# Attention followed by a soft mixture of experts on one core: the V products of a pair gathered in one place, x turned later beside them, the batch softmax steps spread out

## The chip, the cores and the metric

The kernel runs on one core of a Trainium2 chip. A core has five engines that work side by side, each through its own queue in order: TensorE (PE: matrix products and transposes through the array, results in PSUM), VectorE (DVE), ScalarE (ACT), GpSimd (POOL) and SyncE (SP). They wait for each other through semaphores. PSUM has eight banks per core; each holds 512 float32 numbers in each of 128 partitions. The metric is the device time of one execution in microseconds (us). All numbers come from one profiled execution of the kernel before and from three timed runs of it.

## What is computed

The first half is an attention whose softmax has an extra one in its denominator, the second half a soft mixture of experts over its result:

```python
# q, k, v: [8, 12, 448, 64] (batch, heads, tokens, width of a head)
scores = scale * q @ k.T
m = max(scores, -1); e = exp(scores - m)
attn = e / (sum(e) + exp(-m) + 1e-9)
x = (attn @ v), heads side by side           # [3584, 768]
logits = x @ phi                              # 32 slots: 8 experts x 4
d = softmax(logits, over the 3584 tokens)     # dispatch
slot_input = d.T @ x                          # [32, 768]
slot_out = relu(slot_input @ w1[e]) @ w2[e]   # per expert
c = softmax(logits, over the 32 slots)        # combine
out = c @ slot_out                            # [3584, 768]
```

## The kernel before

**Pairs, groups, batches, slots.** Two heads make a pair (48 pairs, n = 0..47), three pairs a group (16), six pairs a batch (8, called b). The main loop has a turn s = 0..48 for each pair, called a slot here, in two halves y = 0 and 1; `hs = 2s + y` counts half slots. The order of work on each engine is the order of the text: the schedule is written by hand, no planner reorders it. Different stages of different pairs share a slot:

- `A` (L218): scores for the maxima, some pairs ahead. PE writes scores (L227; the last, half-sized block L237) into a bank of psA, DVE takes the maximum over a row (L231, L240). Seven maxima per slot: the first and second A, two tiles each, lie in half 0, the third (two tiles) and fourth (one) in half 1.
- `W1`, `W2`, `W3`, once per group: POOL negates the maxima (L247), PE turns them (L267, L268), ACT copies them (L273) and makes exp(-m) (L276, L279). W2 and W3 are in half 1 of each slot with s = 2, 5, 8, ...
- `Bk` (L283): scores again for pair s into psB (L302), the negative maximum added by a second product (L305), ACT takes the exponential (L308). Blocks 0 and 1 in half 0 (four exponentials), 2 and 3 in half 1 (three).
- `T` (L195): PE turns q and k of pair s + 6 (28 transposes, L205) into a psA bank, in half 1; ACT copies it out for the first pair of a group (L208), DVE for the other two (L210).
- `AV` (L327): the V products of a pair (L339), 24 for the three full blocks of queries and 8 for the half-sized one (index 3), summed in one bank of psV. The blocks i = 0, 1 of keys are multiplied in half 1 of the pair's own slot, the rest in half 0 of the next.
- `N1` (L345): ACT copies the sums out (L351). `N2` (L354), in half 1 of the slot after the pair's: DVE makes the divisors (L360, L361), POOL multiplies (L367, L375, L376) and so writes x.
- `PX` (L390): PE turns x of pair s - 2 (four products, L399) into a psB bank, in half 1, and ACT copies it (L405) to xT.
- `P(b)` (L413): the steps of the batch softmax. l_mm makes the logits of the batch (24 products L434; ACT copy L438, DVE maximum L442); l_turn turns them (L450, L452) and c_sub subtracts on POOL (L457); s_max spreads the maxima (L462 to L465), d_sub subtracts on POOL (L469); exps takes exponentials on ACT (L474, L479) and corr rescales the sums on POOL (L480); s_mm sums d.T @ x (28 products L489, DVE sum L499); c_turn turns c (L494, L495). `late(b)` is true for b < 6.

**Banks.** psA has three banks for scores for maxima, T and the steps of P; psB has four for Bk, W2 and PX; psV one. A tile takes the bank of the tile three (four, one) before it, and PE waits until that one has been read.

**Other work of POOL.** POOL also copies V into place (L314 to L317, at the end of slots 0, 3, 6, ...) and issues all loads: v (L145, L146), q and k (L141), the experts' weights (L108). Behind the loop the last batch's steps, the experts and the output follow; the change does not touch these, apart from where they begin.

The positions of the steps of P in half slots, counted from slot 6b + 8, are 0, 1, 2, 4, 6, 9 (s_mm last) for late batches, and 0, 1, 2, 4, 5, 7 for b = 6.

Of the kernel before, what the change touches and what calls it, by code (L numbers as in the profile page):

```python
# [31 lines left out]
def kernel(  # L32
# [20 lines left out]
    PB = H // 2  # L53
    NPAIR = B * PB
# [67 lines left out]
    with ExitStack() as at:  # L122
# [62 lines left out]
        mx, ngm, ec, mT, eT, av, us = {}, {}, {}, {}, {}, {}, {}  # L185
        qkT = {}
        st = {"e2": 0}
# [133 lines left out]
        def av_tile(n):  # L321

            if n >= NPAIR - 3 and n % 2:
                return psA.tile([128, 512], F32, tag="a", name="ps_av")
            return psV.tile([128, 512], F32, tag="v", name="ps_av")

        def AV(n, i, qs):  # L327
            g, pl = divmod(n, NP)
            if i == 0 and qs[0] == 0:
                av[n] = av_tile(n)  # L330
            a = av[n]
            for u in qs:
                for hl in range(2):
                    if u < 3:
                        c0 = (2 * u + hl) * W65
                        o, qc = a[:, c0:c0 + W65], slice(u * 128, (u + 1) * 128)
                    else:
                        o, qc = a[64 - 64 * hl:128 - 64 * hl, 6 * W65:7 * W65], slice(384, 448)
                    nc.tensor.matmul(o, eT[n, i, hl][:, qc], vp[g % 2][:, 2 * pl + hl, i, 0:W65],  # L339
                                     start=(i == 0 and u == 0 and hl == 0),  # L340
                                     stop=(i == 3), skip_group_check=True)

        on_pool = lambda n: n < NPAIR - 4

        def N1(n):  # L345
            src = av[n][:, 0:7 * W65].rearrange("p (s c) -> p s c", c=W65)
            if n == NPAIR - 1:
                us[n] = src
                return
            u = ubuf[:, n % 2, :].rearrange("p (s c) -> p s c", c=W65)  # L350
            (nc.scalar.copy if on_pool(n) else nc.vector.tensor_copy)(u, src)  # L351
            us[n] = u

        def N2(n):  # L354
            g, pl = divmod(n, NP)
            b, pb = divmod(n, PB)
            u = us[n]
            eng = nc.gpsimd if on_pool(n) else nc.vector
            rec = psm.tile([128, 7], F32, tag="rec", name="rec", bufs=3)
            nc.vector.scalar_tensor_tensor(rec, u[:, :, D], 1e-9, ec[mg(n)][:, pl, :], op0=ALU.add, op1=ALU.add)  # L360
            nc.vector.reciprocal(rec, rec)  # L361
            x = xb[b % 2]
            c = pb * 128
            rec2 = psm.tile([128, 2], F32, tag="rec2", name="rec2", bufs=3)
            if n == NPAIR - 1:
                nc.vector.tensor_scalar(rec2, halfm, rec[:, 6:7], None, op0=ALU.mult)
            eng.tensor_mul(  # L367
                x[:, 0:3, c:c + 128].rearrange("p i (h d) -> p i h d", h=2),
                u[:, 0:6, 0:D].rearrange("p (i h) d -> p i h d", h=2),
                rec[:, 0:6].rearrange("p (i h) -> p i h", h=2).unsqueeze(3).to_broadcast([128, 3, 2, D]))  # L370
            if n == NPAIR - 1:
                for h in range(2):
                    nc.scalar.mul(x[:, 3, c + 64 * h:c + 64 * h + 64], u[:, 6, 0:D], rec2[:, h:h + 1])
                return
            eng.tensor_scalar(rec2, halfm, rec[:, 6:7], None, op0=ALU.mult)  # L375
            eng.tensor_mul(  # L376
                x[:, 3, c:c + 128].rearrange("p (h d) -> p h d", h=2),
                u[:, 6, 0:D].unsqueeze(1).to_broadcast([128, 2, D]),
                rec2.unsqueeze(2).to_broadcast([128, 2, D]))
# [3 lines left out]
        def keep_busy(n):  # L383

            if "idle" not in st:
                st["idle"] = pb_("ps_idle")
            for _ in range(n):
                nc.tensor.matmul(st["idle"], ident, w_sb["w1", 0][:, 0, 0:512], start=True, stop=True)

        def PX(n):  # L390
            b, pb = divmod(n, PB)
            x, c = xb[b % 2], slice(pb * 128, pb * 128 + 128)
            two = n == NPAIR - 1
            pss = [pb_("ps_x") for _ in range(1 + two)]
            for i in range(4):
                if i == 3 and two:
                    keep_busy(1)
                o = (i % 2 if two else i) * 128
                nc.tensor.matmul(pss[i // 2 if two else 0][:, o:o + 128], x[:, i, c], ident if i < 3 else ident2,  # L399
                                 start=True, stop=True)  # L400
            if two:
                nc.scalar.copy(xT[:, pb, 0:256], pss[0][:, 0:256])
                nc.vector.tensor_copy(xT[:, pb, 256:512], pss[1][:, 0:256])
            else:
                nc.scalar.copy(xT[:, pb, :], pss[0])  # L405
# [4 lines left out]
        late = lambda b: b < B - 2  # L410
# [114 lines left out]

        post = {}
        for b in range(B - 1):
            for z, f in enumerate(P(b)):  # L530
                post[2 * (PB * b + PB + 2) + z + (z > 2) + (z > 3 + (not late(b))) + 2 * (z > 4) * late(b)] = f

        ub = ubuf.rearrange("p n c -> p (n c)").bitcast(BF16)
        take = lambda z, n: ub[:, z:z + n]
# [14 lines left out]
        def As(c):  # L549
            for _ in range(min(c, len(runs))):  # L550
                A(*runs.pop(0))
# [23 lines left out]
        for s in range(NPAIR + 1):  # L575
            for y in range(2):
                hs = 2 * s + y
                early = int(hs < 5)
                As(1)
                if s < NPAIR:  # L580
                    Bk(s, 2 * y)
                    As(early)
                    side = int(y == 1 and len(runs) > 0 and runs[0][1] == 3)
                    Bk(s, 2 * y + 1, side)
                    As(1 - side)
                else:
                    As(1)
                if hs == 1:
                    W1(1)
                if hs < 5:  # L590
                    T(hs + 3)
                if y == 0:
                    if 0 <= s - 1:
                        for i in (2, 3):
                            AV(s - 1, i, range(3))
                else:
                    if 2 <= s < NPAIR - 6:
                        T(s + 6)
                    g = (s + 1) // 3
                    if (s + 1) % 3 == 0 and g < NG:  # L600
                        W2(g + 1)
                        W3(g + 1)
                    if s < NPAIR:
                        for i in (0, 1):
                            AV(s, i, range(3))
                if 2 * s + y in post:
                    post[2 * s + y]()
                if y and 0 <= s - 2 < NPAIR - 2:
                    PX(s - 2)
                if y == 0:  # L610
                    if 0 <= s - 1:
                        for i in range(4):
                            AV(s - 1, i, [3])
                        N1(s - 1)
                        if not on_pool(s - 1):
                            N2(s - 1)
                else:
                    if 0 <= s - 1 and on_pool(s - 1):
                        N2(s - 1)
                As(early)  # L620
                if hs == 1:
                    W2(1)
                    W3(1)
                if hs == 4:
                    W1(2)
            g = (s + 9) // 3
            if s % 3 == 0 and g - 2 < NG:
                V(g - 2)
                if s and g - 1 < NG:
                    load(g - 1, "v")  # L630
            if s == 1 or (s and s % 3 == 0):
                if g < NG:
                    load(g, "q")
                    load(g, "k")
            if s % 3 == 1:
                if 1 < (s + 2) // 3 < NG:
                    W1((s + 2) // 3 + 1)
                if s == 1:
                    load(2, "v")
            if s in half_at:  # L640
                load_half(half_at[s], 0, w_tile(half_at[s]))
            if s - 1 in half_at:
                load_half(half_at[s - 1], 1)
            for i, z0, z1 in part_at.get(s, ()):
                load_part(i, z0, z1)
# [63 lines left out]
        for half in range(2):  # L709
            for bp in range(B // 2):  # L710
                o = (half * (B // 2) + bp) * 4
                nc.tensor.matmul(ps_cs[:, o:o + 4], cT[:, bp, half, :, :].rearrange("p b j -> p (b j)"), band,
                                 start=True, stop=True)
# [7 lines left out]
        for half in range(2):  # L721
            hs = slice(half * ND, (half + 1) * ND)
# [61 lines left out]
```

## Time and profile before

| What | Value |
|---|---|
| Median of three runs | 328.88 us (327.84 to 330.64) |
| The profiled execution, its own time | 327.88 us |
| Its span, first to last instruction | 326.1 us |
| PE busy | 283.2 us, 87% |
| DVE busy | 252.6 us, 77% |
| ACT busy | 251.5 us, 77% |
| POOL busy | 200.3 us, 61% |
| Row maxima, L231 and L240, DVE | 288 of 613 ns, 48 of 615 ns |
| Exponentials L308, ACT | 336, mean 557 ns |
| V products L339, PE | 1536, 65.0 us busy |
| Granted clock of PE in the loop | 1.00 |

The span is the time between the profile's first and last instruction, the execution's time is a little longer than it. Busy times of one engine overlap with those of another, and neighbouring instructions of one engine overlap too (maxima of 0.61 us follow each other every 0.53 us), so that a cadence, from one start to the next, says more than a duration. In a line of the timeline the columns are: start, length of the group, engine, line, operation, written and read tile with their shapes, number of instructions; in brackets the idle time of that engine before it and what ended it.

### The profile page before, as it was taken

To read this page: it belongs to the slowest core of one execution; us is meant where nothing else is said; L and a number is where in the kernel's file an instruction comes from. 1 tells how busy PE (TensorE), PEld (TensorE's weight loads), DVE (VectorE), ACT (ScalarE), POOL (GpSimd) and SP (SyncE) were. 2 spreads that over 40 slices of the span, in tenths; PEclk is the share of its full clock that TensorE was granted. 3 is DMA by queue.
4 is the path that set the end of the run, shared out by engine and by line. 5 is a ranking of instruction groups with operands and counts; after the bars stand their busy time and mean duration, and the time that the engine had idled before them with its cause. 6 is when DMAs were issued, how large, how long until landed. Compare 5 with 4: busy or idle time off the path is not lost.

```text
span 326.1 us, 12146 instructions
## 1 busy us (share of the span) xinstructions
PE 283.2 (87%) x5074; PEld 162.6 (50%) x5074; DVE 252.6 (77%) x575; ACT 251.5 (77%) x546; POOL 200.3 (61%) x402
## 2 busy tenths in 40 slices
PE   2898999999999999899999999999899997977800
PEld 1444465565665566556655665565555554541100
DVE  5789999998798979798989889888798364326910
ACT  2466699999898999899898989898899993306800
POOL 8651778779587959595979597958766823000000
PEclk9999999999999999999999999999999999987555
DMA  6990899999999999569999999999536999963997
GB/s 87 139 134 2 123 207 155 200 178 178 173 153 166 176 187 146 83 88 181 145 196 154 198 140 199 147 196 140 84 50 98 148 158 192 199 111 150 441 422 338
DMA packets 42438, 54.30 MB, mean 166 GB/s; under 512 B 2576, under 2 KB 35344, under 8 KB 42000
## 3 DMA queue, kind: packets, MB, share of 16 engines
q0 software_dynamic: 41376, 42.52, 84.1%
q1 hardware_dynamic: 1008, 11.01, 8.0%
q8 instruction: 39, 0.64, 0.8%
q14 instruction: 15, 0.12, 0.1%
HBM read 85.03 MB, written 11.01 MB: 295 GB/s over the span
## 4 chain that ended last, share of the span: by engine, by line
PE 37%; DVE 17%; POOL 16%; DMA 12%; ACT 7%; issue 6%; POOLq 0%; ACTq 0%; DVEq 0%
DVE mx L231 11%; DMA R<-in_k_dram 8%; PE ps_av L339 8%; PE ps_b L302 7%; PE ps_a L227 5%; PE ps_b L305 5%; DMA R<-in_moe_w_dram 4%; PE ps_t L205 4%; POOL R L141 3%; POOL R L367 2%; ACT R L308 2%; PE ps_o L742 2%; POOL R L247 2%; ACT W L748 2%; DVE mx L240 2%
## 5 line engine op out<-in xcount | busy, mean ns | idle before, releaser
L231 DVE TENSOR_REDUCE mx<-ps_a 128x1 f32<-128x448 f32 x288 | 160.2, 613 | 14.0 <-PE ps_a L227 13.6
L308 ACT ACTIVATE R<-ps_b 128x448 bf16<-128x448 f32 x336 | 158.0, 557 | 13.5 <-PE ps_b L305 9.9
L302 PE MATMUL ps_b<-R 64*128 64x448 bf16 (+1 forms) x384 | 82.4, 358 | 1.5 <-ACT R L405 1.2
L305 PE MATMUL ps_b<-mT,sel 64*128 64x448 bf16 (+1 forms) x384 | 79.0, 352 | 0.0
L227 PE MATMUL ps_a<-R 64*128 64x448 bf16 x288 | 68.9, 363 | 5.5 <-DVE mx L231 3.1
L367 POOL TENSOR_TENSOR R<-ubuf,rec 128x384 bf16<-128x384 f32 x44 | 36.3, 825 | 48.1 <-ACT R L405 22.4
L339 PE MATMUL ps_av<-R 128*128 128x65 bf16 (+1 forms) x1536 | 65.0, 196 | 0.4 <-issue 0.2
L339 PEld LDWEIGHTS <-R 128*128 128x128 bf16 (+1 forms) x1536 | 50.3, 100 | 23.7 <-issue 19.5
L205 PEld LDWEIGHTS <-R 64*64 64x64 bf16 x1344 | 31.3, 113 | 19.3 <-issue 6.2
L205 PE MATMUL ps_t<-ident,R 64*64 64x64 bf16 x1344 | 32.1, 197 | 7.5 <-DMA R<-in_q_dram 4.2
L302 PEld LDWEIGHTS <-R 64*128 64x128 bf16 (+1 forms) x384 | 19.6, 96 | 30.3 <-issue 25.6
L305 PEld LDWEIGHTS <-sel 64*128 64x128 bf16 (+1 forms) x384 | 21.4, 97 | 22.2 <-issue 15.0
L405 ACT CAST R<-ps_x 128x512 bf16<-128x512 f32 x47 | 27.8, 591 | 3.4 <-PE ps_x L399 3.1
L240 DVE TENSOR_REDUCE mx<-ps_a 128x1 f32<-128x448 f32 x48 | 29.5, 615 | 0.4 <-PE ps_a L237 0.3
L208 ACT COPY R<-ps_t 128x896 bf16<-128x896 bf16 x20 | 18.3, 915 | 12.4 <-PE ps_t L205 12.4
L351 ACT COPY ubuf<-ps_av 128x455 f32<-128x455 f32 x44 | 25.1, 570 | 1.2 <-PE ps_av L339 1.0
L227 PEld LDWEIGHTS <-R 64*128 64x128 bf16 x288 | 17.8, 94 | 14.4 <-issue 3.6
L376 POOL TENSOR_TENSOR R<-ubuf,rec 128x128 bf16<-128x128 f32 x44 | 17.5, 398 | 3.7
L237 PE MATMUL ps_a<-R 64*64 64x448 bf16 x96 | 18.5, 381 | 0.6 <-DVE mx L231 0.6
L399 PE MATMUL ps_x<-ident,R 128*128 128x128 bf16 x192 | 18.7, 218 | 0.0
L108 POOL DMA_DIRECT2D R<-in_moe_w_dram x15 | 10.7, 714 | 12.7 <-PE ps_s L489 5.3
L247 POOL TENSOR_SCALAR R<-mx 64x6 bf16<-64x6 f32 (+5 forms) x51 | 13.5, 264 | 8.2 <-DVE mx L231 4.7
(126 smaller groups left out, 363.8 us busy)
## 6 DMA issues: line engine op xcount, KB each, us to landing
W<-in_moe_w_dram POOLq DMA_DIRECT2D x22, 768.0 KB, 9.0
out_dram<-W SPq DMA_DIRECT2D x3, 2688.0 KB, 11.2
R<-in_v_dram POOLq DMA_DIRECT2D x32, 192.0 KB, 4.0
R<-in_q_dram POOLq DMA_DIRECT2D x15, 336.0 KB, 6.7
R<-in_k_dram POOLq DMA_DIRECT2D x15, 336.0 KB, 7.7
R<-in_moe_w_dram POOLq DMA_DIRECT2D x3, 768.0 KB, 8.4
out_dram<-W SPq DMA_DIRECT2D x3, 768.0 KB, 4.3
R<-in_moe_w_dram POOLq DMA_DIRECT2D x1, 1344.0 KB, 11.7
```

What stands on the lines that cost most here:

```text
L205: nc.tensor.transpose(ps[r, a, c:c + 64], src[r, pl, tok * D:(tok + 1) * D], ident[r, r])
L227: nc.tensor.matmul(pss[hl][:, 0:S], t[r, 0, i * 128:(i + 1) * 128], t[r, 1, :], start=True, stop=True)
L231: nc.vector.reduce_max(mx[g][:, c:c + 1], pss[hl][:, 0:S], axis=AX.X)
L240: nc.vector.reduce_max(mx[g][:, c:c + 1], ps[:, 0:S], axis=AX.X)
L247: neg = lambda o, s: nc.gpsimd.tensor_scalar(o, s, -1.0, None, op0=ALU.mult)
L302: nc.tensor.matmul(outs[hl], t[rs[hl], 1, cols], t[rs[hl], 0, :], start=True, stop=False)
L305: nc.tensor.matmul(outs[hl], sel[rs[hl], 2 * pl + hl:2 * pl + hl + 1].to_broadcast([64, m]), mT[mg(n)][rs[hl], :], start=False, stop=True)
L308: nc.scalar.activation(e, p[:, 0:S], AF.Exp, scale=scale)
L339: nc.tensor.matmul(o, eT[n, i, hl][:, qc], vp[g % 2][:, 2 * pl + hl, i, 0:W65], start=(i == 0 and u == 0 and hl == 0), stop=(i == 3), skip ...
L351: (nc.scalar.copy if on_pool(n) else nc.vector.tensor_copy)(u, src)
L367: eng.tensor_mul(x[:, 0:3, c:c + 128].rearrange("p i (h d) -> p i h d", h=2), u[:, 0:6, 0:D].rearrange("p (i h) d -> p i h d", h=2), rec[: ...
L405: nc.scalar.copy(xT[:, pb, :], pss[0])
```

## The change

- All 32 V products of a pair now stand in half 0 of the slot after the pair's own: first the half-sized block of queries (index 3) for all four blocks of keys, then the full blocks. The copy N1 follows at once. Only the last pair (47) keeps its first two blocks of keys in its own slot. As the first product into the bank is now another, the flag that starts the sum (`start`) goes by the first block multiplied.
- x of pair s - 3 is turned in half 0 of slot s, behind N1 and the step of P, for pairs up to 40 (`TURN`); the later ones stay at s - 2 in half 1.
- The steps of P for late batches stand at half slots 2, 4, 6, 8, 10 (s_mm) and 11 (c_turn) behind slot 6b + 8, in half 0 apart from c_turn; in half 0 they now come behind N1. For b = 6 they stay at 0, 1, 2, 4, 5, 7.

```diff
         def AV(n, i, qs):
             g, pl = divmod(n, NP)
-            if i == 0 and qs[0] == 0:
+            if n not in av:
                 av[n] = av_tile(n)
+                st["first"] = qs[0]
...
-                                     start=(i == 0 and u == 0 and hl == 0),
+                                     start=(i == 0 and u == st["first"] and (u == 3 or hl == 0)),
...
+        TURN = NPAIR - 8
         post = {}
         for b in range(B - 1):
-            for z, f in enumerate(P(b)):
-                post[2 * (PB * b + PB + 2) + z + (z > 2) + (z > 3 + (not late(b))) + 2 * (z > 4) * late(b)] = f
+            for at_s, f in zip((2, 4, 6, 8, 11, 10) if late(b) else (0, 1, 2, 4, 5, 7), P(b)):
+                post[2 * (PB * b + PB + 2) + at_s] = f
...
                 if y == 0:
                     if 0 <= s - 1:
-                        for i in (2, 3):
+                        done = 2 * (s == NPAIR)
+                        for i in range(4):
+                            AV(s - 1, i, [3])
+                        for i in range(done, 4):
                             AV(s - 1, i, range(3))
+                        N1(s - 1)
+                        if not on_pool(s - 1):
+                            N2(s - 1)
+                    if hs in post:
+                        post[hs]()
+                    if 0 <= s - 3 <= TURN:
+                        PX(s - 3)
                 else:
...
-                    if s < NPAIR:
+                    if s == NPAIR - 1:
                         for i in (0, 1):
                             AV(s, i, range(3))
-                if 2 * s + y in post:
-                    post[2 * s + y]()
-                if y and 0 <= s - 2 < NPAIR - 2:
-                    PX(s - 2)
-                if y == 0:
-                    if 0 <= s - 1:
-                        for i in range(4):
-                            AV(s - 1, i, [3])
-                        N1(s - 1)
-                        if not on_pool(s - 1):
-                            N2(s - 1)
-                else:
+                    if hs in post:
+                        post[hs]()
+                    if TURN < s - 2 < NPAIR - 2:
+                        PX(s - 2)
+                if y:
                     if 0 <= s - 1 and on_pool(s - 1):
                         N2(s - 1)
```

## The prediction

> **What bounds the kernel now.** I read the page first: engines and slices. PE, DVE and ACT are busy 87, 77 and 77% of 326.1 us and nearly level from 40 to 265 us. So no engine is simply the limit, and a slot (one pair's turn of the loop) has to be read from the timeline. The slots are cut at the first score product of L302: slot 36 begins at 210.82, 37 at 216.01, 38 at 220.57. In the windows view the batch of slots 33 to 38 (195.29 to 226.83) takes 31.54 us; PE is busy 30.11 of them, ACT 28.96, DVE 28.07, POOL 24.73.
>
> Timeline of DVE, slots 36 to 38 (start, length, line, what, how many; idle time before in brackets):
>
> ```profile
> 211.02 3.32 DVE L231 TENSOR_REDUCE mx<-ps_a 128x1 f32<-128x448 f32 x6 [0.76 <-PE ps_a L227]
> 214.25 0.62 DVE L240 TENSOR_REDUCE mx<-ps_a 128x1 f32<-128x448 f32 x1
> 215.76 0.39 DVE L499 TENSOR_TENSOR acc<-acc,ps_s 128x224 f32<-128x224 f32 x1 [0.89 <-PE ps_s L489]
> ...
> 216.37 3.23 DVE L231 TENSOR_REDUCE mx<-ps_a 128x1 f32<-128x448 f32 x6
> 219.52 0.61 DVE L240 TENSOR_REDUCE mx<-ps_a 128x1 f32<-128x448 f32 x1
> 220.05 0.61 DVE L210 COPY R<-ps_t 128x896 bf16<-128x896 bf16 x1
> 220.58 0.15 DVE L360 SCALAR_TENSOR_TENSOR rec<-ubuf,ec 128x7 f32<-128x7 f32 x1
> 220.77 0.20 DVE L361 RECIPROCAL rec<-rec 128x7 f32<-128x7 f32 x1
> 220.89 1.65 DVE L231 TENSOR_REDUCE mx<-ps_a 128x1 f32<-128x448 f32 x3
> ```
>
> From 216.37 to 220.89 DVE has no gap: seven row maxima 0.53 us apart, the copy of the turned q and k, two small divisions. That is 4.52 us, and the slot takes 4.56: **DVE sets a plain slot**, where nothing holds it up. Where something does, the brackets say so: 0.76 behind the products W2 (L267, L268), 0.89 behind s_mm (L489).
>
> Timeline of PE over the same slot, and over the end of slot 35:
>
> ```profile
> 209.25 0.34 PE L267 MATMUL ps_m<-ident,R 128*128 128x128 bf16 x3
> 209.90 0.20 PE L268 MATMUL ps_m<-ident,R 128*128 128x64 bf16 x1 [0.31 <-POOL R L247]
> ...
> 216.77 0.57 PE L227 MATMUL ps_a<-R 64*128 64x448 bf16 x2
> 217.28 0.79 PE L339 MATMUL ps_av<-R 128*128 128x65 bf16 x20
> 217.99 0.41 PE L227 MATMUL ps_a<-R 64*128 64x448 bf16 x2
> ...
> 219.68 0.54 PE L339 MATMUL ps_av<-R 128*128 128x65 bf16 x12
> 220.06 0.39 PE L399 MATMUL ps_x<-ident,R 128*128 128x128 bf16 x4
> 220.37 0.36 PE L227 MATMUL ps_a<-R 64*128 64x448 bf16 x2
> ```
>
> See where the V products (L339) lie: 20 between the second and third scores for the maxima (L227), 12 and the turning of x after the last. psA has three banks, so the second score tile's second product (217.00: the group ends at 217.34, one lasts 0.35) waits for the slot's first maximum, begun at 216.37: 0.63 after it. The next scores start 0.99 later, and a maximum follows its product by 0.40 (210.62 to 211.02). So the third maxima could start at 0.63 + 0.99 + 0.40 = 2.02 us into DVE's slot; the first four end at 4 x 0.525 = 2.10. PE is in time by 0.08.
>
> **Cost, part by part.** (a) *V products together.* The 12 of half 1 move into half 0, between the second and third scores. Their cadence is (0.54 - 0.20)/11 = 0.031 us, so 0.37. A run of 32 isn't in the trace: at least 0.37, at most twelve lone products of 0.196 (2.35); the pipelined row is nearest. (b) *x turned next to them:* four products, (0.39 - 0.22)/3 = 0.057 apart, 0.23. Together 0.60, so the third maxima can start at 2.62, not 2.02. DVE has nothing queued in between and **idles 0.52 us in every slot**. After it come three maxima (1.59), the copy (0.53, in two slots of three; each third one is on ACT) and the divisions (0.31): 5.05 us a slot instead of 4.52, and 4.52 instead of 4.49 (slot 3) where ACT copies. PE is then ahead in half 1: behind the transposes (L205) it has only the next scores, 1.2 us before DVE needs them. This hides W2 and its wait.
>
> (c) *ACT.* In half 0 ACT now has four exponentials, the copy of the V products (L351) and that of x (L405, 0.59); in half 1 three exponentials and, each third slot, the copy L208 (0.93). By the same walk this copy runs from 4.55 to 5.48 in its slot; the next slot's second scores take its bank and wait until 5.53, where they would be wanted at 4.52 + 0.63 = 5.15: +0.37 behind each such slot. Before has its like: in slot 4 the second scores wait on L405, and the slot takes 4.96. Three plain slots: 4.52 + 5.42 + 5.05 = 14.99.
>
> (d) *Steps of the batch softmax.* Steps now in half 0 lengthen the same stretch of PE: l_mm 0.62 (24 products, and ACT's copy that its maximum follows), l_turn 0.14, s_max 0.15, s_mm 0.71 (L489 to L399 in slot 36: 214.80 to 215.50). Their small DVE work falls into the idle stretch. c_turn in half 1 adds its copy, 0.13. The exponentials (0.43 on ACT) fall into a slot with L208 and make its wait 0.84 instead of 0.37: +0.47. L208 behind l_mm costs 0.27 less, DVE being late there already. Sum 0.62 + 0.14 + 0.14 + 0.71 + 0.13 + 0.47 - 0.27 = 1.94. A batch: 2 x 14.99 + 1.94 = **31.92**, against 31.41, the mean of slots 8 to 37 (63.54 to 220.57 is 157.03).
>
> (e) *What goes.* W2's wait for POOL, the 0.76 and 0.89 above, and ACT's L405 in PE's way in slot 4: all inside the 31.41, replaced by the idle 0.52. POOL: from the division of slot 33 to the third L247 it works through 200.18 to 209.85 without a real pause (two rounds of N2, V, four transfers issued, corr, W1). corr (0.65) leaves this queue for slot 6b+12, where POOL sat idle 3.4 us; c_sub (0.41) enters. No DMA is issued elsewhere in the order. If POOL came 0.5 late at W2, the 1.2 above covers 0.5; without that cover it is 14 x 0.5 = 7 us. Transposes waited 1.04 (slot 39) and some 0.7 to 0.9 (slots 12, 21) for q and k; as T now comes 0.60 later in its slot, I keep 1.2 of these 2.7, between 0 and 2.7.
>
> *Sum:* slots 3 to 7 24.93 against 23.99, +0.94; five batches +2.6; slots 38 to 41 20.67 against 22.22, -1.55; transfers +1.2; slots 42 and 43, which have maxima but no transposes, 9.9 against 8.62, +1.25 (s_mm now falls into 43); slots 0 to 2, same stretch, denser scores, +0.4 (0 to 1); after slot 43 the work lies as before, or is ACT's: 0 +- 0.5. Total +4.8. The profiled execution took 327.88; **332.7**. The median shown is 328.88, so that is 1.2% over it; 1% is about what this measurement can tell from no change.
>
> **Another way to count.** PE changes between products of different tiling six times a slot, and each change costs 0.09: transposes to V products 0.13 where neighbours are 0.03 apart, x to scores 0.31 - 4 x 0.057. The change leaves five, but gives W2 its own in 14 slots: 39 x 0.09 - 14 x 0.09 = 2.3 us less on PE, worth something only where PE sets the slot. The Trainium skill (TensorEngine Tiling, Tiling Modes) says that changing the tiling mode drains the TensorE; the trace agrees with its 0.09. By that rule alone the sum would be 325.6.
>
> **Rivals.** *Faster, 322 to 326:* PE sets the slot. For it: PE's 30.11 of 31.54; POOL's wait at W2 (0.43 in slot 35, 14 times, 6 us, where PE is the limit) goes, the mode changes with it. Against: slot 37 is DVE's to 0.04 us, and the 0.08 of spare is less than the 0.60 moved. It decides if DVE comes to the third score with over 0.5 us queued, which three banks don't allow while 0.63 is a bank wait. 327.88 - 2.3 - 2 (a third of the W2 waits) = 323.6; chance 0.22.
> *No difference, 327 to 331:* the idle 0.52 comes, but both W2's waits and those for q and k vanish whole and L208 isn't late: 4.8 - 1.2 - 12 x 0.2 = +1.2, 329.1; chance 0.18.
> *Much slower, 335 to 340:* ACT doesn't catch up after L208. ACT has 29.0 us of work in 31.9; if its lag passes to the slot behind as well (0.37 more, 13 times), it is 332.7 + 4.8 = 337.5. For it: L405 already held PE in slots 4 and 34. Against: ACT would have some 0.8 free in a slot of 5.05. Chance 0.18.
> That the order isn't what the text says is no rival: each engine's order is written out by hand.
>
> **How the numbers follow.** Forecast 332.7, 330.5 to 335, chance 0.42: 0.29 of it over 332.2 (1% over the median), 0.13 under. Slower: 0.29 + 0.18 = 0.47. Same: 0.13 + 0.18 = 0.31. Faster: 0.22. The range goes from 325.5, leaving out most of the faster case, to 338, leaving out the end of the worst.
>
> **What would show it.** Right: a gap of about 0.5 on DVE before each third score maximum (none in slot 37 now), released by L227; DVE periods of about 5.05 and 4.52; W2 without cost to DVE; slot 6b+13 near 6.7 us with s_mm; one run of 32 products L339 ending in L399. Wrong: DVE without such gaps; POOL still last at L268 with DVE idle behind it; ACT idle ahead of L208; or PE slots of 4.4 us.

## The result and the profile after

The changed kernel is slower, by less than the forecast: 329.71 us median against 329.27 of before in 20 runs each, with a ratio of 1.006 (95% interval 1.0034 to 1.0085). In a later comparison it was 330.41 against 327.62, ratio 1.0111 (1.0056 to 1.0165). The forecast was 332.7, 1.2% over the median shown. Both intervals lie above 1; only the second reaches 1.2%.

Some executions of either kernel are disturbed and take over 1.5% longer than its fastest ones, so all ratios here are of the undisturbed ones, and the profile used for the changed kernel is its second (span 328.5 us, its execution 330.27 us), as the first is of a disturbed execution. Behind line 330 of the changed kernel the line numbers are one or more higher than in before: L340 is the V products (was L339), L361 and L362 the divisions, L400 the turning of x, L500 the sum behind s_mm.

Timeline of DVE in the second profile of the changed kernel, slots 36 and 37 and the start of 38 (columns as before):

```profile
214.99 2.17 DVE L231 TENSOR_REDUCE mx<-ps_a 128x1 f32<-128x448 f32 x4
217.60 1.16 DVE L231 TENSOR_REDUCE mx<-ps_a 128x1 f32<-128x448 f32 x2 [0.44 <-PE ps_a L227]
218.67 0.61 DVE L240 TENSOR_REDUCE mx<-ps_a 128x1 f32<-128x448 f32 x1
219.21 0.15 DVE L361 SCALAR_TENSOR_TENSOR rec<-ubuf,ec 128x7 f32<-128x7 f32 x1
...
219.51 2.19 DVE L231 TENSOR_REDUCE mx<-ps_a 128x1 f32<-128x448 f32 x4
...
225.95 2.16 DVE L231 TENSOR_REDUCE mx<-ps_a 128x1 f32<-128x448 f32 x4
228.57 1.16 DVE L231 TENSOR_REDUCE mx<-ps_a 128x1 f32<-128x448 f32 x2 [0.46 <-PE ps_a L227]
```

The run of six maxima is now cut after the fourth: 0.44 and 0.46 us in which DVE waits for the third scores. The fifth maximum, the first of the third scores, starts 2.61 us behind the first one in slot 36 (214.99 to 217.60) and 2.62 in slot 38 (225.95 to 228.57); the prediction has 2.62. Slot 37 (219.51 to 225.95) is the one with s_mm. Timeline of PE for slot 38:

```profile
226.42 0.52 PE L227 MATMUL ps_a<-R 64*128 64x448 bf16 x2
226.87 1.15 PE L340 MATMUL ps_av<-R 128*64 128x65 bf16 x32
227.86 0.39 PE L400 MATMUL ps_x<-ident,R 128*128 128x128 bf16 x4
228.18 0.36 PE L227 MATMUL ps_a<-R 64*128 64x448 bf16 x2
...
229.81 0.34 PE L267 MATMUL ps_m<-ident,R 128*128 128x128 bf16 x3
229.99 0.19 PE L268 MATMUL ps_m<-ident,R 128*128 128x64 bf16 x1
```

Here are the run of 32 and the four of x, right between two groups of L227; L268 has no wait in brackets any more. What ended PE's idle time at L268, the profile before and the second one after:

```profile
  POOL R L247: 7.6, 20
```

```profile
  POOL R L247: 1.3, 5
```

These figures count the weight load and the product of L268 each; the products alone waited 2.95 us in 10 waits before and not at all after. So the wait for POOL went as foreseen, and a wait of DVE took its place.

Where the 2.4 us between the two spans lie, by the start of the slots (cut at L302, as in the prediction):

| Stretch | Before | After | Difference | Foreseen |
|---|---|---|---|---|
| slots 0 to 2 | 25.05 | 26.70 | +1.65 | +0.4 |
| slots 3 to 7 | 23.99 | 24.52 | +0.53 | +0.94 |
| slots 8 to 37 | 157.03 | 159.94 | +2.91 | +2.6, and up to 1.2 of waits for q and k |
| slots 38 to 41 | 22.22 | 20.26 | -1.96 | -1.55 |
| slots 42, 43 | 8.62 | 9.82 | +1.20 | +1.25 |
| slots 44 to 46 | 13.63 | 14.33 | +0.70 | 0 |
| slot 47 to the first product of the experts | 13.43 | 12.47 | -0.96 | 0 |
| experts and output | 47.63 | 45.97 | -1.66 | 0 |

The loop from slot 3 to 46 gives +3.38 us; the differences in the first three slots and in the experts go with the granted clock (last section).

### The profile page after: what moved, and what is told of

Same layout as the page of the kernel before. It is cut to its first block, busy times and chain, and to the rows that moved or that the text cites. A ratio compares the mean times of both kernels' runs of the same rounds, so it can differ in the third digit from the quotient of the medians.

```text
span 331.0 us, 12131 instructions
## 1 busy us (share of the span) xinstructions
PE 288.1 (87%) x5072; PEld 163.6 (49%) x5074; DVE 252.9 (76%) x575; ACT 250.4 (76%) x546; POOL 200.7 (61%) x402
## 4 chain that ended last, share of the span: by engine, by line
PE 45%; DVE 15%; ACT 12%; DMA 9%; POOL 8%; issue 6%; POOLq 0%; ACTq 0%
PE ps_av L340 11%; PE ps_a L227 8%; DVE mx L231 8%; PE ps_b L305 6%; PE ps_b L302 6%; DMA R<-in_k_dram 6%; ACT R L308 6%; DMA R<-in_moe_w_dram 4%; PE ps_t L205 3%; DVE mx L240 3%; PE ps_o L751 2%; ACT mT L273 2%; ACT W L757 2%; PE ps_x L400 2%; DVE R L210 2%
## 5 line engine op out<-in xcount | busy, mean ns | idle before, releaser
L308 ACT ACTIVATE R<-ps_b 128x448 bf16<-128x448 f32 x336 | 158.1, 559 | 23.9 <-PE ps_b L305 22.3
L231 DVE TENSOR_REDUCE mx<-ps_a 128x1 f32<-128x448 f32 x288 | 160.3, 612 | 16.9 <-PE ps_a L227 16.2
L227 PE MATMUL ps_a<-R 64*128 64x448 bf16 x288 | 75.7, 372 | 11.3 <-DVE mx L231 4.0
L302 PE MATMUL ps_b<-R 64*128 64x448 bf16 (+1 forms) x384 | 80.8, 365 | 0.6
L305 PE MATMUL ps_b<-mT,sel 64*128 64x448 bf16 (+1 forms) x384 | 76.8, 359 | 1.3
L340 PEld LDWEIGHTS <-R 128*128 128x128 bf16 (+1 forms) x1536 | 47.4, 100 | 25.4 <-issue 22.9
L340 PE MATMUL ps_av<-R 128*128 128x65 bf16 (+1 forms) x1536 | 55.6, 195 | 0.1
L205 PEld LDWEIGHTS <-R 64*64 64x64 bf16 x1344 | 31.3, 114 | 18.3 <-issue 5.6
L302 PEld LDWEIGHTS <-R 64*128 64x128 bf16 (+1 forms) x384 | 21.8, 97 | 35.0 <-issue 31.4
L205 PE MATMUL ps_t<-ident,R 64*64 64x64 bf16 x1344 | 32.8, 199 | 6.5 <-DMA R<-in_q_dram 4.2
L305 PEld LDWEIGHTS <-sel 64*128 64x128 bf16 (+1 forms) x384 | 25.7, 98 | 20.0 <-issue 10.4
L406 ACT CAST R<-ps_x 128x512 bf16<-128x512 f32 x47 | 28.4, 605 | 1.7 <-PE ps_x L400 1.7
L208 ACT COPY R<-ps_t 128x896 bf16<-128x896 bf16 x20 | 18.4, 918 | 11.1 <-PE ps_t L205 10.9
L227 PEld LDWEIGHTS <-R 64*128 64x128 bf16 x288 | 17.3, 95 | 19.0 <-issue 7.4
L400 PE MATMUL ps_x<-ident,R 128*128 128x128 bf16 x192 | 18.7, 218 | 0.0
```

Of the source, the lines that this page charges most:

```text
L205: nc.tensor.transpose(ps[r, a, c:c + 64], src[r, pl, tok * D:(tok + 1) * D], ident[r, r])
L227: nc.tensor.matmul(pss[hl][:, 0:S], t[r, 0, i * 128:(i + 1) * 128], t[r, 1, :], start=True, stop=True)
L231: nc.vector.reduce_max(mx[g][:, c:c + 1], pss[hl][:, 0:S], axis=AX.X)
L302: nc.tensor.matmul(outs[hl], t[rs[hl], 1, cols], t[rs[hl], 0, :], start=True, stop=False)
L305: nc.tensor.matmul(outs[hl], sel[rs[hl], 2 * pl + hl:2 * pl + hl + 1].to_broadcast([64, m]), mT[mg(n)][rs[hl], :], start=False, stop=True)
L308: nc.scalar.activation(e, p[:, 0:S], AF.Exp, scale=scale)
```

## Experiments

Each ran beside the kernel before on the same chip, in three comparisons on three chips; ratios are to that neighbour, so rows with different neighbours are compared by their ratios. "Idle of DVE" is summed by what followed it, over slots 26 to 37 (two batches), from all gaps over 0.05 us (the timeline prints those over 0.15). Theory 1 is that of the prediction: DVE's maxima set the slot, three banks let PE be only so far ahead, and what lies between the second and third scores empties them. Theory 2: PE sets the slot, with its changes of tiling.

| Kernel | Median, before beside it | Ratio (95%) | Batch, slots 32 to 37 |
|---|---|---|---|
| changed, again | 330.41, 327.62 | 1.0111 (1.0056 to 1.0165) | 31.79 |
| V products gathered alone | 332.56, 327.62 | 1.0167 (1.0122 to 1.0212) | 31.78 |
| all but the gathering | 325.12, 327.62 | 0.9945 (0.9914 to 0.9976) | 31.35 |
| steps alone | 325.72, 327.62 | 0.9934 (0.9894 to 0.9974) | 31.07 |
| third scores amid the V products | 335.05, 327.95 | 1.0258 (1.0210 to 1.0306) | 32.73 |
| the same, x in half 1 | 340.76, 327.95 | 1.0399 (1.0345 to 1.0453) | 33.37 |
| V products of pairs 0 to 2 split | 329.45, 327.95 | 1.0064 (1.0029 to 1.0099) | 31.81 |
| four banks for maxima, three for exponentials | 350.39, 327.95 | 1.0698 (1.0641 to 1.0755) | 35.01 |
| 12 products more, half 0 | 346.40, 328.83 | 1.0552 (1.0499 to 1.0606) | 34.47 |
| 12 products more, half 1 | 332.92, 328.83 | 1.0113 (1.0051 to 1.0174) | 31.86 |
| all but the gathering, steps first | 324.79, 328.83 | 0.9878 (0.9831 to 0.9925) | 31.01 |

Before has 31.52 in the same six slots.

**The changed kernel again.**

> The changed kernel once more, for its ratio beside the others and for a second profile. Theory 1 (three banks of psA: DVE stands idle before the third score maximum of each slot, PE has time to spare in half 1): ratio 1.003 to 1.009, batches of about 31.8 us in the loop, idle 0.2 to 1.2 us on DVE before the third maximum. In the first profile PE's granted clock came to full only at 27.2 us and fell again at 34.1 us, where before had it from 18.4 us on; if this belongs to the change (slot 0 has no V products any more), it is seen again here and slots 0 to 2 take about 27.5 us; if it is chance, slots 0 to 2 take about 25 us.

Measured: batches of 31.77 to 31.79 in slots 20 to 37 (32.25 and 32.34 in the two before these). Idle of DVE: 2.38 us ahead of the third maximum, 2.44 ahead of the sum behind s_mm, 1.62 ahead of l_mm's maximum, 0.47 ahead of l_turn's: 6.91 together against 6.25 in before, where it lay elsewhere (2.61 ahead of the first maximum, 1.78 s_mm, 1.11 l_turn, 0.41 l_mm, 0.35 second maximum). Ahead of the sum behind s_mm the profile names POOL as the last release: in slot 37 its copy of V (L316) ends at 222.87 and s_mm at 222.81, so that this wait isn't shown to be PE's alone. The ratio, 1.0111, lies above the expected 1.003 to 1.009, though its interval reaches into it. The start is dealt with below.

**Which part costs.** Three kernels with one or two parts of the change each. In `gather_only` the places of x and of the steps are those of before:

```diff
-        TURN = NPAIR - 8
+        TURN = -1
-            for at_s, f in zip((2, 4, 6, 8, 11, 10) if late(b) else (0, 1, 2, 4, 5, 7), P(b)):
+            for at_s, f in zip((0, 1, 2, 4, 6, 9) if late(b) else (0, 1, 2, 4, 5, 7), P(b)):
```

> Only the V products are gathered (N1 behind them); x is turned at s - 2 in half 1 and the steps of the batch softmax stand as before. Theory 1: 12 products of 0.031 us come into the stretch between second and third scores, DVE idles 0.3 us a slot there, W2's wait on POOL is partly hidden: base of three slots 14.5 us as before, ratio 0.995 to 1.005. Theory 2 (PE sets the slots, its changes of tiling decide: one less per slot): ratio 0.99 to 0.995, and no idle time on DVE before the third maximum.

Idle ahead of the third maximum came (0.37 in plain slots, 0.3 foreseen), which theory 2 doesn't have; but the ratio, 1.0167, is outside what either expected. The rest is in the slots behind an ACT copy of q and k. Timelines of PE and of ACT at the start of slot 4 of this kernel:

```profile
45.52 0.35 PE L302 MATMUL ps_b<-R 64*128 64x448 bf16 x1
46.57 0.35 PE L302 MATMUL ps_b<-R 64*128 64x448 bf16 x1 [0.70 <-ACT R L406]
```

```profile
45.10 0.93 ACT L208 COPY R<-ps_t 128x896 bf16<-128x896 bf16 x1
45.88 0.63 ACT L406 CAST R<-ps_x 128x512 bf16<-128x512 f32 x1
```

x is turned right behind the transposes now, its copy L406 stands behind L208 on ACT, and PE waits 0.70 us for its bank: slot 4 takes 5.80 us by DVE's clock, 5.22 in the changed kernel and 5.07 in before. All such waits of L302 for L406 sum to 4.0 us in 8 waits here, and the changed kernel has none. So the first part of the change needs the second: x turned in half 0 takes this wait away.

`no_gather` is the change without its first part:

```diff
-                        done = 2 * (s == NPAIR)
+                        for i in (2, 3):
+                            AV(s - 1, i, range(3))
                         for i in range(4):
                             AV(s - 1, i, [3])
-                        for i in range(done, 4):
-                            AV(s - 1, i, range(3))
...
-                    if s == NPAIR - 1:
+                    if s < NPAIR:
                         for i in (0, 1):
                             AV(s, i, range(3))
```

> The change without its first part: V products split over two half slots as before, but x turned three slots behind in half 0, N1 ahead of the steps, the steps two half slots apart. Theory 1: only x's turning (0.23 us) and the steps lengthen the stretch, DVE idles 0.15 us a slot, batches of 30.4 us, ratio 0.98 to 0.99: the gathering is the part that costs. Theory 2: six changes of tiling as before, so no slot is shorter, ratio 0.998 to 1.01.

Faster than before, 0.9945, as theory 1 has it and theory 2 not, but by half of what was expected: the batch takes 31.35, 30.4 were expected. Much of the miss is the loads: 1.40 us of idle time ahead of the first maximum in slots 31 and 37 come behind transposes that waited 0.26 and 0.55 us for k from DMA (slots 30 and 36). PE's waits for q and k in slots 3 to 41 sum to 2.73 us here, to 0.98 in the changed kernel and to nothing in the slower `extra_h0` below. Idle ahead of the third maximum is 0.18 to 0.20 in a plain slot (0.15 expected, 0.44 with the gathering). Dropping the gathering alone takes the changed kernel from 1.0111 to 0.9945.

`posts_only` is before with the table (0, 4, 6, 8, 11, 10) for the steps:

> Before with only the steps of the batch softmax moved: l_mm stays at 0, the others at 4, 6, 8, 10 (s_mm) and 11 (c_turn), in their old place inside a half slot. Theory 1: s_mm no longer holds the divisors that POOL waits for ahead of W1 (0.89 idle on DVE in slot 36), corr leaves POOL's queue ahead of W1: 0.3 us a batch less, ratio 0.99 to 0.997. Theory 2: same work on PE, ratio 0.998 to 1.002.

0.9934, inside the expectation. Idle of DVE ahead of the sum behind s_mm fell from 1.78 to 0.46 and the 1.11 ahead of l_turn's maximum went. So of the three parts, the steps gain 0.7% by themselves and the gathering loses more than that. What x alone does wasn't run.

**The same work in two places.** Twelve constant products of the V products' size and one change of tiling, put into slots 3 to 41 of the changed kernel; their sums are never read. In `extra_h0` (shown) they stand ahead of the V products, in `extra_h1` the same products, into the bank that has been copied out, stand in half 1 behind the transposes and W2:

```diff
+                        if 3 <= s < NPAIR - 6:
+                            av[s - 1], st["first"] = av_tile(s - 1), 3
+                            for j in range(12):
+                                nc.tensor.matmul(av[s - 1][:, (j % 7) * W65:(j % 7 + 1) * W65], ident,
+                                                 ident[:, 0:W65], start=True, stop=True, skip_group_check=True)
```

> The changed kernel with twelve more products of the size of a V product (constants, written into the V products' bank ahead of them and cleared by their first product) in half 0 of slots 3 to 41, between the second and the third scores: 12 x 0.031 us and one change of tiling, 0.46 us of PE a slot. Theory 1: all of it is on the loop through DVE, 39 x 0.46 = 18 us longer than the changed kernel, ratio to before 1.055 to 1.075, idle time ahead of the third maximum up by 0.4 a slot. Theory 2 (PE sets every slot): 18 us as well.

> The changed kernel with the same twelve products and the same extra change of tiling in half 1 of slots 3 to 41, behind the transposes and W2, ahead of the step of the batch softmax. Theory 1: there PE is 1.2 us ahead of DVE where DVE copies q and k (26 of the slots), 0.3 where ACT does; so nothing in the first and 0.16 in each of the others, 0 to 4 us in all, ratio to before 1.005 to 1.02. Theory 2: PE has the same 0.46 more a slot, 18 us, ratio 1.055 or more.

The two together tell the theories apart: the ratios are 1.0552 and 1.0113. Timelines of DVE in slot 32, changed kernel, `extra_h0`, `extra_h1`:

```profile
196.78 1.15 DVE L231 TENSOR_REDUCE mx<-ps_a 128x1 f32<-128x448 f32 x2 [0.46 <-PE ps_a L227]
```

```profile
209.33 1.15 DVE L231 TENSOR_REDUCE mx<-ps_a 128x1 f32<-128x448 f32 x2 [0.93 <-PE ps_a L227]
```

```profile
197.49 1.16 DVE L231 TENSOR_REDUCE mx<-ps_a 128x1 f32<-128x448 f32 x2 [0.46 <-PE ps_a L227]
```

In half 0 all of it is on the loop: the idle time grows by 0.47 (0.46 put in) and slots 3 to 41 take 221.59 us against 204.71, +16.9 (18 expected). In half 1 it is hidden: slot 32 keeps its 5.07 us, slot 36, where ACT copies, goes from 4.52 to 4.71 (0.16 expected); slots 26 to 37 take 64.08 against 63.56. Slots 3 to 41 take 208.24, +3.5 (0 to 4 expected, 18 by theory 2); 3.3 of it are four pauses of PE (1.19, 1.08, 0.69 and 0.37 us in slots 15, 16, 25 and 27) for which the profile shows no wait and which the changed kernel doesn't have. Where they come from is open. Timeline of PE in `extra_h1`, where the twelve lie (L621):

```profile
198.91 0.19 PE L268 MATMUL ps_m<-ident,R 128*128 128x64 bf16 x1
198.94 0.53 PE L621 MATMUL ps_av<-ident 128*128 128x65 bf16 x12
199.40 0.36 PE L227 MATMUL ps_a<-R 64*128 64x448 bf16 x2
```

PE's next scores begin at 199.40, and DVE takes them at 199.94, when it has finished its own work. PE doesn't set the slot. The Trainium skill (TensorEngine Tiling, Tiling Modes) has every change of tiling mode drain the TensorE; the trace agrees with 0.09 us each, but in half 1 one more of them cost nothing. In slot 32 the twelve share the tiling of W2; slot 34 has no W2, so that they bring a change of their own, and its period is 5.25 against 5.36.

**Moving the third scores.** If the stretch is the trouble, the third scores could go into the middle of the V products (`after_mid`), where they are issued as early as in before:

```diff
-                As(1)
+                if y == 0 or s < 3:
+                    As(1)
...
                         for i in range(done, 4):
+                            if i == 2 and s >= 3:
+                                As(1)
                             AV(s - 1, i, range(3))
```

> The changed kernel with the third score tile of a slot (which was the first work of half 1) put between the second and third block of keys of the gathered V products. Theory 1 (the stretch of PE between second and third scores empties the three banks): the idle time ahead of the third maximum, 2.36 us in slots 26 to 37 and 4.05 more behind steps that lie in the same stretch, falls to under 0.3; some of it comes back ahead of the fourth maximum, 0.2 a slot and 0.6 behind l_mm and s_mm; PE changes its tiling twice more a slot (0.19). Batches of 30.5 to 31.2 instead of 31.8, ratio to before 0.985 to 1.0. Theory 2 (PE and its changes of tiling set the slot): 12 x 0.095 = 1.1 us a batch longer, ratio 1.02 or more.

A miss. Idle ahead of the third maximum did fall, from 2.38 to 1.32, but 4.06 us of it now lie ahead of the fourth, and 1.41 ahead of the second, where PE waits for ACT: in slots 33 and 36 for the copy of the turned maxima (L273, 0.47 and 0.41), in slot 37 for L208 (0.24). That is 7.34 together instead of 6.91. The batch is 0.94 longer. Timeline of DVE, slot 34:

```profile
208.72 2.22 DVE L231 TENSOR_REDUCE mx<-ps_a 128x1 f32<-128x448 f32 x4
211.21 1.16 DVE L231 TENSOR_REDUCE mx<-ps_a 128x1 f32<-128x448 f32 x2 [0.27 <-PE ps_a L227]
...
212.85 0.62 DVE L240 TENSOR_REDUCE mx<-ps_a 128x1 f32<-128x448 f32 x1 [0.29 <-PE ps_a L237]
```

Twelve of the V products, the step and x now stand between the third and the fourth scores, and the fourth come too late. By number theory 2 (1.1 us a batch) fits this run as well; the pair above doesn't allow it as the general rule. Theory 1 had the wait ahead of the fourth about right (0.2 a slot and 0.6 behind l_mm and s_mm, 4.0 in all); it missed the waits for ACT, the 1.32 that stayed, and 1.35 us of overlap between DVE's instructions that are lost (last section). The variant with x in half 1 and the steps at (0, 4, 6, 8, 11, 10), `mid_px1`:

> The V products gathered around the third scores as in after_mid, x turned at s - 2 in half 1, steps of the batch softmax at 0, 4, 6, 8, 10 (s_mm), 11. Theory 1: the work of PE between scores is spread so that DVE always has tiles: 30.0 to 30.8 a batch, ratio 0.975 to 0.99, better than posts_only's 0.993. Theory 2: at least 1.01.

A miss too, 1.0399: 3.33 us ahead of the second maximum (PE waits 9.7 us in all for L406), 1.81 ahead of the fourth, 1.66 ahead of the first.

**Four banks.**

```diff
-        psA = pool("psA", 3, space=PSUM)
-        psB = pool("psB", 4, space=PSUM)
+        psA = pool("psA", 4, space=PSUM)
+        psB = pool("psB", 3, space=PSUM)
```

> The changed kernel with four banks for scores for maxima (psA) and three for the exponentials (psB), instead of three and four. Theory 1: with four banks PE gets one tile further ahead, so the idle time of DVE ahead of the third maximum in slots 26 to 37 falls from 2.36 us to under 1; what three psB banks cost shows as PE waiting for L308 (exponentials) and L406, and may eat the gain: ratio to before 0.99 to 1.03. Theory 2: the idle time ahead of the third maximum stays.

A miss, 1.0698, and it settles nothing: PE now waits 23.0 us for the exponentials' banks, and the idle ahead of the third maximum, 2.86, can come from these waits. That three banks hold PE back is seen elsewhere. The second product of the second scores takes the bank that the first maximum has read, and in slots 3 to 41 of the changed kernel it never starts sooner than 0.05 us behind that maximum's end, in 21 of the 39 slots just there; in before the least is 0.05 too. What a fourth bank would give stays open.

**The start.** Pairs 0 to 2 as in before (`after_warm`):

```diff
-                        done = 2 * (s == NPAIR)
+                        done = 2 * (s == NPAIR or s <= 3)
...
-                    if s == NPAIR - 1:
+                    if s == NPAIR - 1 or s < 3:
```

> The changed kernel, but the pairs 0 to 2 keep their first two blocks of V products in their own slots, as before. If the late clock of the changed kernel (full at 27.2 and 27.6 us in two profiles, 18.4 to 19.0 in before and in the two kernels with split V products) comes from a slot 0 without V products, full clock is back by 19 us and slots 0 to 2 take 25.0 to 25.3 us instead of 26.7 to 27.6, 1.5 us off the whole. If it is chance, slots 0 to 2 stay near 26.7 in this run or the clock is late in runs without the change as well.

The profile does show the early clock and 25.01 us. It doesn't settle the cause: see the last section. The ratio, 1.0064, lies between the changed kernel's two, so that the 1.5 us can't be seen in it.

**A faster version.** `no_gather` with the step of the batch softmax ahead of the half-sized block and of N1:

```diff
+                    if hs in post:
+                        post[hs]()
+                    if 0 <= s - 1:
                         for i in range(4):
                             AV(s - 1, i, [3])
                         N1(s - 1)
                         if not on_pool(s - 1):
                             N2(s - 1)
-                    if hs in post:
-                        post[hs]()
```

> No_gather with the step of the batch softmax ahead of the half-sized block's V products and of N1, as in before: ACT's copy of the logits no longer waits behind N1, so DVE's 1.51 us ahead of its maximum (slots 26 to 37) fall to about 0.6. Theory 1: 0.4 us a batch less than no_gather, ratio 0.985 to 0.995. Theory 2: one or two changes of tiling more in six slots, no gain.

0.9878: faster than both kernels. Timelines of DVE, `no_gather` and this one, slot 33:

```profile
198.39 0.29 DVE L443 TENSOR_REDUCE cm<-ps_l 128x4 f32<-128x128 f32 x1 [0.76 <-ACT lb L439]
```

```profile
197.80 0.29 DVE L443 TENSOR_REDUCE cm<-ps_l 128x4 f32<-128x128 f32 x1 [0.31 <-ACT lb L439]
```

Two such fell from 1.51 to 0.61, as expected. Its batch of slots 32 to 37 is 31.01 against 31.35, but slots 26 to 37 take 62.43 against 62.51: in slot 30 the transposes waited 0.80 us for k, 0.26 in `no_gather`. That it is faster than `no_gather` or `posts_only` isn't shown, as the intervals overlap.

## Why the prediction was right, and where its sizes were off

**Direction and place: right.** The changed kernel is slower, and the time is lost where the prediction has it: ahead of the third scores, in a gap that the work of PE moved there makes. The size of the whole is less well met. The forecast is the profiled execution plus 4.8 us, 1.5%; the ratios are 0.6% and 1.1%, and both medians of the changed kernel (329.71, 330.41) lie in the band of "no difference" (327 to 331) and just under the forecast's own (330.5 to 335). DVE's periods, taken from its first maximum of a slot to the next, second profile:

| Slot | 3, 4, 5 | 6b+8 | 6b+9 | 6b+10 | 6b+11 | 6b+12 | 6b+13 | Sum |
|---|---|---|---|---|---|---|---|---|
| foreseen | 4.52, 5.42, 5.05 | 5.06 | 5.14 | 5.30 | 5.20 | 4.52 | 6.74 | 31.96 |
| after (slots 32 to 37) | 4.51, 5.22, 5.06 | 5.07 | 5.11 | 5.36 | 5.30 | 4.52 | 6.43 | 31.79 |

The "foreseen" of single slots is the prediction's walk laid out: 5.05 or 4.52, plus each step's own figure; rounding leaves 0.04 to its 31.92.

**(a), (b)** The third scores' first maximum comes 2.61 to 2.62 us into the slot, foreseen 2.62. The idle time shown is 0.44 to 0.46 and not 0.52, because the maximum ahead of the gap no longer overlaps with the next one (last section). The run of 32 takes 0.99 from its first product to the first of x (226.87 to 227.86), at the pipelined cadence chosen, not at that of lone products.

**(c)** L208's lag was mis-sized: slot 4 is 0.16 longer than slot 5, not 0.37, and 6b+13 0.31 shorter than foreseen. In slot 3 the copy starts 4.33 us behind the first maximum (41.89 to 46.22), not 4.55, and that is about the 0.21 by which the lag is shorter. Over slots 3 to 7, with slots 4 and 7, this makes the difference between +0.94 and +0.53.

**(d)** l_mm, l_turn, s_max, s_mm and c_turn cost what the walk gave to within 0.1 us a slot, when the 0.21 of (c) is taken off 6b+13; `posts_only` confirms that their new places are a gain where the V products stay split.

**(e)** W2's wait went, and with it DVE's 2.61 us ahead of the first maximum; `extra_h1` shows that the spare time of PE behind the transposes is real. Of the waits of L205 for q and k, 2.2 us in before (0.69, 0.49 and 1.04 in slots 12, 21 and 39; the prediction's 2.7 is somewhat high), 0.98 stayed (0.73 in slot 12, 0.25 in slot 24), 1.2 foreseen; the first profile of the changed kernel has 1.58. Slots 38 to 43 came as foreseen to 0.5 us.

**What failed is the sum's last step**, "the work lies as before" behind slot 43. It doesn't: only pair 47 keeps two blocks in its own slot, so the V products of the pairs before it are gathered there too. Slots 44 to 46 are 0.70 longer and the way from slot 47 to the experts 0.96 shorter. The first of these belongs to the gathering: slots 44 to 46 take 14.33 us or more in every profile with gathered V products and 13.24 to 13.63 in the four with split ones. The second stays open, as it is 12.46 to 12.92 us in the gathered and 12.03 to 14.46 in the split ones. The granted clock differs besides: the first slots have +1.65 and the experts -1.66 in these two profiles, which cancel by luck. Slots 3 to 46 were foreseen at +4.4 (with the 1.2) and are +3.4; with the -0.96 behind them that is +2.4 us, 0.7%. The two comparisons (0.6% and 1.1%) lie on either side of it, and single runs of the changed kernel spread from 327.86 to 332.81.

**The rivals.** "Faster" fell with `extra_h1`: PE isn't the limit. "Much slower" fell too: ACT catches up within a slot. "No difference" holds the same idle time as the forecast and differs from it in the smaller terms only. It came nearer to the amount (+1.2 against +4.8, +2.4 measured), and half of its reasons came true: the waits for q and k fell from 2.2 to 1.0 us and L208's lag from the foreseen 0.37 to 0.16. So the runs bear out the mechanism that the two share and lie between their sizes.

## What to carry to other kernels

Where an engine eats tiles from a few PSUM banks, look at how long the feeding engine is away between two tiles, not at its total work: 0.46 us of added products cost 0.47 in one place and nothing some 3 us later in the same slot (0.92 and 4.07 us behind the first maximum of slot 32). Gathering work that shares a mode saves the changes of mode, but makes that absence longer; spread it so that no absence exceeds what the banks hold. Here that is 1.07 us: PE can write its fourth tile 0.63 us behind the first maximum, the first four maxima end at 2.10, and a maximum follows its product by 0.40. From that product to the next scores PE was away 0.99 before and 1.59 with the 0.60 added, and the third scores came 0.52 late. And before moving the eaten tile instead, check what then stands before the next one.

## What the runs showed of the hardware that was not expected

**The clock of TensorE at the start differs from profile to profile.** Timelines of PE, first block product of slot 0's second half: before, changed kernel (second profile), `extra_h1` and `no_gather_first`:

```profile
19.62 0.37 PE L302 MATMUL ps_b<-R 64*128 64x448 bf16 x2
```

```profile
19.92 0.60 PE L302 MATMUL ps_b<-R 64*128 64x448 bf16 x2
```

```profile
19.50 0.37 PE L302 MATMUL ps_b<-R 64*128 64x448 bf16 x2
```

```profile
19.93 0.60 PE L302 MATMUL ps_b<-R 64*128 64x448 bf16 x2
```

The same pair of products takes 0.37 or 0.60 us. Full clock came at 18.4 us in before, at 27.6 in the changed kernel, but at 18.1 in `extra_h1`, whose slots 0 to 2 are those of the changed kernel, at 18.6 in `gather_only`, whose slot 0 has no V products either, and at 23.9 in `no_gather_first`, whose V products are split as in before. Slots 0 to 2 took 24.40 to 27.55 us over all profiles. So the +1.65 can't be put down to the change; whether fewer products in slot 0 make the late clock likelier stays open. Behind the loop the clock differs too. In before it fell to half 26.4 us behind the start of slot 47, came back for 3.4 us and fell again; in the changed kernel it fell once, 30.6 us behind it. The experts had 31.2 us of half clock in before and 27.8 in the changed kernel, and there the 1.66 us are: over all profiles they take 45.6 to 46.8 us with at most 28.5 us of half clock and 47.2 to 48.7 with 30.7 or more. The Trainium skill (TensorE: Matmul & The Clock Gate, The HAM clock gate) describes a window of activity of about 3.4 us that runs free of the kernel's start, so that the same kernel meets it at different points; the records here agree, with stretches of 3.4 us (before), 6.8 (first profile of the changed kernel) and 13.7 (`gather_only`). The same section of the Trainium skill has the moment of full clock vary by some 500 ns from run to run; here it differs by 9.5 us between profiles with the same slots 0 to 2, `extra_h1` and the changed kernel.

**A cut run of maxima costs more than the gap.** In a run, maxima follow each other every 0.53 us, a lone one takes 0.61. So the gap of 0.44 us in slot 36 puts the fifth maximum 0.53 us back: it starts 2.61 us behind the first, and 2.08 in slot 37 of before, which has no gap. DVE's time outside idle gaps over slots 26 to 37 was 56.65 us in the changed kernel and 58.12 in `after_mid`, with more gaps and the same instructions: neighbours overlap by 7.90 us in the one and by 6.55 in the other.
